# Gate pieces of a token group at other half steps of the dense layers, in a chain of attention, dense layers and a mixture of experts

## The chip, the core and the metric

One core of a Trainium2 chip runs the whole program. The metric is the device time of one execution, in microseconds (us). The engines are named as the profile names them: PE (TensorE, the matrix engine) and PEld (its weight loads), DVE (VectorE), ACT (ScalarE), POOL (GpSimd), SP (SyncE, which here only issues DMAs).

## The reference

Three stages follow one another on 4608 tokens of width 512. The attention stage works in chunks of 64 tokens; the dense stage is two layers; the last is a mixture of 8 experts with a noisy gate that picks two of them for each token.

```python
attn = softmax(scale * q_c @ k_c.T);  x = attn @ v_c          # chunks of 64 tokens, 8 heads of 64
...
h = x @ w_in                                                   # 512 -> 2048
x = (h - np.tanh(h)) @ w_out                                   # 2048 -> 512
...
noise_scale = np.log1p(np.exp(x @ w_noise))
noisy_logits = x @ w_gate + noise_scale * noise
top2 = ...                                                     # two largest of 8, softmax weights
for e in range(E):
    out[mask] += top2_w[mask] * (relu(x[mask] @ w1[e]) @ w2[e])  # 512 -> 1024 -> 512
```

## The kernel before

**Tiling.** The 4608 tokens are 36 tiles of 128. They form 11 groups g0 to g10 of 4 or 3 tiles (4, 3, 4, 3, 4, then 3 each). The dense layers of a group run in 16 steps, one for each 128 columns of the hidden layer, and each step has two half steps: the first layer (`layer1`, 12 matmuls of L327 into `hp`, which has two buffers) and the second layer of the step before (`layer2`, three matmuls for each tile, L399, into `acc`, four PSUM banks). So a group has 32 half steps, numbered 0 to 31; an even one is behind a first layer, an odd one behind a second. Numbers are 32-bit floats split in a high and a low part, three passes each. Between the layers `activate` forms h - tanh(h): the tanh on ACT (L347), the subtraction on DVE (L350), the cast of the high part on ACT (L351), the low part on DVE (L353). The second layer of the step needs both parts, and L350 also frees the bank of `hp`.

**What runs beside them.** Each half step has a list of other work (`at(h, fn, ...)`), which is recorded behind that half step's matmuls and what follows them, on all engines. The order within an engine is the order of recording; nothing rearranges it. In these lists stand the attention of later tiles (`u_attn` and its softmax pieces, L172 to L180 on DVE), the loads and transposes of tiles of x, and the gate of the group before: while group g is in its dense layers, the gate of group g-1 is computed. Its pieces are `u_lg` (logits on PE), `u_gate` (L487 on, exp), `u_gate2` (start of the series for log1p), `u_gate2a` (the series: eight terms in L519, the last in L520, all on DVE), `u_gate2b` (noise and top-2, L528 to L537 on DVE), `u_gate2c` (exp on ACT), `u_gate3` (weights and one-hot, POOL and DVE) and `u_pos` (place of each token in its expert's list, two matmuls and ten DVE operations, then the scatters).

**Scatters.** `u_pos` puts into the queue `waiting` one `reload` for each tile, and behind those the short entries of the lists. A `reload` loads a tile `yr` from `x2d` and puts a pair of scatters of it, `xs<-yr` (L602), into `loaded`. `issue`, called twice in each step, lets them out: POOL copies a mark into `spacer` (L376), which waits until ACT (L369) or DVE (L371) has written that mark in `activate`, then sends all that is in `loaded`, then takes one thunk from `waiting`. The ACT mark is only written when something waits at that time.

**End of a group.** The second layer of the last step runs inside the first step of the next group. Behind it `store_y` copies the banks of `acc` into tiles `y`, even ones on ACT (L443), odd ones on DVE (L441), and SP stores them to `x2d` (L444). Later `u_z` and `u_yt` load and transpose them for the gate. The tiles `y`, `z`, `x2t`, `yr` and `o` share one ring of four buffers (the tag "y"), so each waits until the last reader of the buffer is done.

Of the kernel before, what the change touches and what calls it, by code (L numbers as in the profile page):

```python
# [15 lines left out]
ALU = mybir.AluOpType  # L16
# [14 lines left out]
def moe_chain_kernel(ctx: ExitStack, tc: tile.TileContext, q, k, v, w_in, w_out, wgn, noise,  # L31
                     w1, w2, out):
    nc = tc.nc
    NT = q.shape[0]
    NTOK = NT * 128
    GS = SIZES or [4, 3] * 3 + [3] * ((NT - 21) // 3)
    NG = len(GS)
# [392 lines left out]
    GT = {}  # L430
# [70 lines left out]
    def u_gate2(g):  # L501
# [11 lines left out]
        ve.tensor_scalar(u, s2, 2.0 / (2 * n_terms + 1), None, op0=ALU.mult)  # L513
        GT[g] = lg, u, t, s2, n_terms, nz

    def u_gate2a(g):
        lg, u, t, s2, n_terms, nz = GT[g]
        for m in range(n_terms - 1, 0, -1):
            nc.vector.scalar_tensor_tensor(u, u, 2.0 / (2 * m + 1), s2, op0=ALU.add, op1=ALU.mult)  # L519
        nc.vector.scalar_tensor_tensor(u, u, 2.0, t, op0=ALU.add, op1=ALU.mult)  # L520
        GT[g] = lg, u, nz
# [350 lines left out]
    def L(f, *a):  # L872
        return lambda: f(*a)
# [107 lines left out]
    def at(h, fn, *a):  # L981
        slots[h].append(L(fn, *a))
# [15 lines left out]
    for g in range(1, NG - 1):  # L998
        hs = (1, 5, 9, 14, 18, 23) if g == 1 else (5, 9, 15, 21) if GS[g + 1] > 3 else (5, 14, 20)
# [11 lines left out]
    for g in range(NG):  # L1011
        h0 = H1 * g
        at(h0, load_nz, g)
        if g > 0:
            n = GS[g - 1]
            for j in range(n):
                i = G0[g - 1] + j
                at(h0 + 1 + j, u_z, i)
                at(h0 + 5 + j, u_yt, i)

            h = h0 + (11 if g + 1 < NG and GS[g + 1] > 3 else 9)
            at(h, u_lg, g - 1)
            h += 2
            for d, fn in zip((0, 2, 3, 4, 6, 7, 12), (u_gate, u_gate2, u_gate2a, u_gate2b,
                                                      u_gate2c, u_gate3, u_pos)):
                at(h + d, fn, g - 1)
        if g == 0:
            at(H1 + 6, sums)
            at(26, store_consts)
            for o, f in ((0, 3), (1, 2), (1, 3)):  # L1030
                at(0, fetch_w, o, f)
            for f in range(NF1):
                at(2 * f, fetch_w, 0, f + 4)
                if f:
                    at(2 * f, prep_w, 1, f)
                at(2 * f, decode_w, 0, f + 2)
                at(2 * f, rebias_w, 0, f + 3)
                at(2 * f + 1, fetch_w, 1, f + 4)
                at(2 * f + 1, prep_w, 0, f + 2)
                at(2 * f + 1, decode_w, 1, f + 1)  # L1040
                at(2 * f + 1, rebias_w, 1, f + 2)
        else:
            for f in range(0, NF1):
                if g == 1:
                    if f < E:
                        at(h0 + 2 * f, zero_x, 2 * f)
                        at(h0 + 2 * f, zero_x, 2 * f + 1)
                elif (g - 2) * NF1 + f < NT + DUMMY // 128:
                    at(h0 + 2 * f, zero_out, (g - 2) * NF1 + f)
        if g == NG - 1:  # L1050
            at(h0 - 4, u_cum)
            at(h0 - 2, u_bump)
            at(h0 + 12, load_list0)
            for c in range(min(3, SEAL // 128)):
                at(h0 + 8 + 3 * c, fetch_x, 0, c)
            for c in range(g0[1]):
                at(h0 + min(21 + 4 * c, H1 - 1), first_xt, c)
            for f in range(NF2):
                at(h0 + 2 * f + 7, fetch_e, 0, f)
                at(h0 + 2 * f + 10, prep_e, 0, f)  # L1060
# [26 lines left out]
    for gi, (e, ge, c0, nt, n) in enumerate(groups):  # L1087
        h0 = H1 * NG + H2 * gi
        if gi == 0:
            for j in range(GS[-1]):  # L1090
                at(h0 + 1, u_z, G0[-1] + j)
                at(h0 + 6 + j, u_yt, G0[-1] + j)
            at(h0 + 6 + GS[-1], u_lg, NG - 1)
            h = h0 + 8 + GS[-1]
            for d, fn in zip((0, 1, 1, 2, 3, 3), (u_gate, u_gate2, u_gate2a, u_gate2b,
                                                  u_gate2c, u_gate3)):
                at(h + d, fn, NG - 1)
            at(h + 4, u_cum)
            at(h + 7, u_pos, NG - 1)
            at(h0 + H2 + 3, u_over)  # L1100
            at(h0 + H2 + 7, dispatched)
            at(h0 + 2 * H2 + 2, load_list)
        if gi + 1 == len(groups):
            at(h0 + 8, u_tiles_over)
        else:
            for j in range(groups[gi + 1][3]):
                at(h0 + ((3 + 2 * j, 10 + 2 * j)[gi] if gi < 2 else 1 + 4 * j), xt_unit, gi + 1, j)
        if ge < 2:
            for f in range(4):
                at(h0 + 4 * f, fetch_e, e + 1, 4 * ge + f)  # L1110
                at(h0 + 4 * f + 3, prep_e, e + 1, 4 * ge + f)
# [72 lines left out]
```

## Time and profile before

| | us |
|---|---|
| three runs | 1760.42, 1760.86, 1760.87 |
| median | 1760.86 |
| span of the profiled execution | 1760.4 |
| PE busy in it | 1739.3 (99%) |
| PEld busy | 1489.6 (85%) |
| DVE busy | 791.3 (45%) |
| ACT busy | 547.1 (31%) |
| POOL busy | 492.9 (28%) |

The span is that of one execution, from its first to its last instruction. Matmuls are pipelined, so blocks of them overlap a little in the timeline; how far a block is late is read from the distance between the starts of two blocks. Idle time of the other engines costs nothing unless PE comes to wait for it.

### The profile page before, as it was taken

Reading aid. Unit: us, or ns where it says so; the run is one execution under the profiler, and the core shown is the slowest. Engines: PE = TensorE matmul, PEld = TensorE weight load, DVE = VectorE, ACT = ScalarE, POOL = GpSimd, SP = SyncE. Lnnn points to the kernel's source line nnn. Section 1 sums busy time; section 2 is a strip of 40 time slices with the busy share of each in tenths; the row PEclk is TensorE's granted clock in tenths of the full one; section 3 lists DMA queues with packets and bytes.
Section 4 is the critical chain, followed back from the end, with each engine's and each line's share of the span. In section 5 each row is a group of like instructions: output and inputs, shape, how many; then the busy total and the mean of one; then the engine's idle time right before and its main releaser. Section 6 shows DMA issues by size and latency. Waiting matters only on the chain. (4 is left out here: it accounts for less than half of the span.)

```text
span 1760.4 us, 28384 instructions
## 1 busy us (share of the span) xinstructions
PE 1739.3 (99%) x10791; PEld 1489.6 (85%) x10792; DVE 791.3 (45%) x2070; ACT 547.1 (31%) x1108; POOL 492.9 (28%) x752
## 2 busy tenths in 40 slices
PE   8999999999999999999999999999999999999997
PEld 5788888888888888888888888988898888988886
DVE  7966453645354545544466333433333333343321
ACT  4643322332233323332343323233223223232211
POOL 3650403040304123031353523222232223132112
PEclk9999999999999999999999999999999999999999
DMA  7436435562314222230354543443343343343212
GB/s 292 182 117 176 151 83 143 134 175 66 106 59 137 67 79 91 73 103 25 120 161 114 141 107 78 101 108 65 88 103 102 73 95 91 84 119 71 55 25 36
DMA packets 197830, 184.68 MB, mean 105 GB/s; under 512 B 80176, under 2 KB 139568, under 8 KB 197680
## 3 DMA queue, kind: packets, MB, share of 16 engines
q1 hardware_dynamic: 178064, 142.73, 27.1%
q0 software_dynamic: 19328, 39.41, 11.3%
q8 instruction: 96, 1.57, 0.4%
q10 hardware_dynamic: 288, 0.52, 0.1%
q14 instruction: 54, 0.44, 0.1%
HBM read 118.76 MB, written 63.84 MB: 104 GB/s over the span
## 5 line engine op out<-in xcount | busy, mean ns | idle before, releaser
L327 PE MATMUL hp<-xt,wa 128*128 128x384 f32 (+3 forms) x4416 | 885.5, 349 | 0.6 <-DVE g L350 0.6
L399 PE MATMUL acc<-wb,gt 128*128 128x512 f32 (+1 forms) x3510 | 877.9, 395 | 2.9 <-ACT gt L351 2.4
L327 PEld LDWEIGHTS hp<-xt,wa 128*128 128x128 f32 x4416 | 766.9, 188 | 83.6 <-issue 2.2
L399 PEld LDWEIGHTS acc<-wb,gt 128*128 128x128 f32 (+1 forms) x3510 | 650.2, 188 | 139.3 <-ACT gt L351 3.7
L358 DVE SCALAR_TENSOR_TENSOR gt<-hp,gt 128x384 fp32r<-128x384 f32 (+2 forms) x192 | 113.5, 591 | 469.1 <-ACT gt L355 453.7
L355 ACT ACTIVATE gt<-hp 128x384 fp32r<-128x384 f32 (+2 forms) x192 | 99.4, 518 | 476.9 <-PE hp L327 416.4
L350 DVE TENSOR_TENSOR g<-hp,g 128x384 f32<-128x384 f32 (+1 forms) x176 | 103.8, 590 | 257.7 <-ACT g L347 235.4
L347 ACT ACTIVATE g<-hp 128x384 f32<-128x384 f32 (+1 forms) x176 | 91.5, 520 | 335.2 <-PE hp L327 303.3
L312 POOL TENSOR_TENSOR wb<-st,wb 128x512 fp32r<-128x512 f32 x64 | 92.8, 1451 | 323.1 <-ACT wb L310 323.1
L351 ACT CAST gt<-g 128x384 fp32r<-128x384 f32 (+1 forms) x176 | 95.4, 542 | 164.2 <-DVE g L350 134.4
L376 POOL COPY spacer<-mark 1x1 f32<-1x1 f32 x182 | 46.7, 257 | 346.9 <-DVE mark L371 280.6
L353 DVE TENSOR_TENSOR gt<-g,gt 128x384 fp32r<-128x384 f32 (+1 forms) x160 | 94.8, 592 | 96.1 <-ACT gt L351 86.3
L732 POOL DMA_INDIRECT out_dram<-o,lsa x73 | 119.3, 1634 | 56.7 <-DVE o L729 37.9
L551 POOL TENSOR_SCALAR r<-d 128x3 f32<-128x3 f32 (+1 forms) x11 | 5.1, 461 | 388.5 <-ACT d L542 388.4
L602 POOL DMA_INDIRECT xs<-yr,row x72 | 71.5, 993 | 32.0 <-issue 24.2
L269 DVE TENSOR_TENSOR xt<-xg,xt 128x512 fp32r<-128x512 f32 x80 | 54.3, 679 | 54.4 <-ACT xt L268 53.7
L268 ACT CAST xt<-xg 128x512 fp32r<-128x512 f32 x80 | 48.8, 610 | 93.3 <-DVE xg L449 86.8
L602 POOL DMA_INDIRECT lst<-pay,row x72 | 70.1, 974 | 16.7 <-issue 15.6
L449 DVE STREAM_TRANSPOSE xg<-xg 128x512 f32<-128x512 f32 x80 | 56.4, 704 | 0.0
L312 DVE TENSOR_TENSOR wa<-st,wa 128x512 fp32r<-128x512 f32 x64 | 45.2, 706 | 5.4 <-ACT wa L310 5.3
L310 ACT CAST wa<-st 128x512 fp32r<-128x512 f32 x64 | 39.2, 613 | 4.5 <-DMA st<-in_w_dram 4.5
L310 ACT CAST wb<-st 128x512 fp32r<-128x512 f32 x64 | 39.7, 620 | 0.2 <-DMA st<-in_w_dram 0.2
(195 smaller groups left out, 864.3 us busy)
## 6 DMA issues: line engine op xcount, KB each, us to landing
st<-in_w_dram SPq DMA_DIRECT2D x128, 256.0 KB
xg<-xs SPq DMA_DIRECT2D x320, 64.0 KB
out_dram<-zero SPq DMA_DIRECT2D x40, 256.0 KB
x2d<-y SPq DMA_DIRECT2D x36, 256.0 KB
z<-x2d SPq DMA_DIRECT2D x144, 64.0 KB
yr<-x2d SPq DMA_DIRECT2D x36, 256.0 KB
q<-in_q_dram SPq DMA_DIRECT2D x34, 256.0 KB
v<-in_v_dram SPq DMA_DIRECT2D x34, 256.0 KB
```

What stands on the lines that cost most here:

```text
L310: nc.scalar.copy(w[:, 0, :], x)
L312: eng.tensor_tensor(w[:, 1, :], x, w[:, 0, :].bitcast(F32), op=ALU.subtract)
L327: nc.tensor.matmul(s.hp[:, :m], lhsT=w[:, a, d, :], rhs=s.xt[:, b, d, :m], start=(i == 0), stop=(i == 11))
L347: nc.scalar.activation(g, hp[:, :n], AF.Tanh)
L350: nc.vector.tensor_tensor(g, hp[:, :n], g, op=ALU.subtract)
L351: nc.scalar.copy(hi, g)
L353: eng.tensor_tensor(lo, g, hi.bitcast(F32), op=ALU.subtract)
L355: nc.scalar.activation(hi, hp[:, :n], AF.Relu)
L358: nc.vector.scalar_tensor_tensor(lo, hp[:, :n], 0.0, hi.bitcast(F32), op0=ALU.max, op1=ALU.subtract)
L399: nc.tensor.matmul(s.grp["acc"][j][:m], lhsT=s.gt[:, a, j * 128:j * 128 + m], rhs=s.B[s.f][:, b, :], start=(s.f == 0 and i == 0), stop=(s. ...
L602: s = nc.gpsimd.indirect_dma_start(out=to, out_offset=bass.IndirectOffsetOnAxis(ap=at, axis=0), in_=src, in_offset=None)
L732: a = nc.gpsimd.indirect_dma_start(out=out, out_offset=bass.IndirectOffsetOnAxis(ap=en[:m, 0:1], axis=0), in_=o[:m], in_offset=None, compu ...
```

## The change

The series of `u_gate2a` is cut: a new piece `u_gate2h` does its first four terms, and `u_gate2a` the other four and the last, by the number of terms left. The pieces of the gate stand at other half steps. In the order logits, gate, gate2, gate2h, gate2a, gate2b, gate2c, gate3, pos the half steps were 11, 13, 15, -, 16, 17, 19, 20, 25 for g1 and g3, and 9, 11, 13, -, 14, 15, 17, 18, 23 for the others; now they are in four rows, one each for g10, g1, g3 and the rest. The expert phase, which runs the gate of g10, keeps its own table.

```diff
         n_terms = 9
         ve.tensor_scalar(u, s2, 2.0 / (2 * n_terms + 1), None, op0=ALU.mult)
         GT[g] = lg, u, t, s2, n_terms, nz
+
+    def u_gate2h(g):
+        lg, u, t, s2, n_terms, nz = GT[g]
+        for m in range(n_terms - 1, n_terms - 5, -1):
+            nc.vector.scalar_tensor_tensor(u, u, 2.0 / (2 * m + 1), s2, op0=ALU.add, op1=ALU.mult)
+        GT[g] = lg, u, t, s2, n_terms - 4, nz
 
     def u_gate2a(g):
         lg, u, t, s2, n_terms, nz = GT[g]
@@
-            h = h0 + (11 if g + 1 < NG and GS[g + 1] > 3 else 9)
-            at(h, u_lg, g - 1)
-            h += 2
-            for d, fn in zip((0, 2, 3, 4, 6, 7, 12), (u_gate, u_gate2, u_gate2a, u_gate2b,
-                                                      u_gate2c, u_gate3, u_pos)):
-                at(h + d, fn, g - 1)
+            if g == NG - 1:
+                hs = (9, 11, 12, 14, 16, 18, 20, 20, 23)
+            elif g == 1:
+                hs = (11, 12, 13, 21, 22, 26, 28, 29, 31)
+            elif GS[g + 1] > 3:
+                hs = (11, 12, 13, 18, 19, 24, 26, 28, 30)
+            else:
+                hs = (9, 11, 12, 13, 17, 18, 21, 24, 28)
+            for h, fn in zip(hs, (u_lg, u_gate, u_gate2, u_gate2h, u_gate2a, u_gate2b, u_gate2c,
+                                  u_gate3, u_pos)):
+                at(h0 + h, fn, g - 1)
```

The first place is DVE in the middle of group 3 (the gate of group 2). Before, from the series on; L172 to L180 are the softmax of an attention tile, L528 to L535 the top-2 piece, which goes on with three more pairs of L534 and L535 and L537 before the next L350:

```order
L519 SCALAR_TENSOR_TENSOR u<-u,s_3804 128x32 x8
L520 SCALAR_TENSOR_TENSOR u<-u,t 128x32
L172 TENSOR_REDUCE sm<-e 128x8
L176 TENSOR_SCALAR sm<-sm 128x8
L177 RECIPROCAL sm<-sm 128x8
L180 TENSOR_TENSOR e<-e,sm 128x512
L528 SCALAR_TENSOR_TENSOR u<-lg,u 128x32
L529 TENSOR_TENSOR u<-u,nz 128x32
L530 TENSOR_TENSOR u<-u,lg 128x32
L534 MAX m_3856<-u 128x8
L535 MAX_INDEX i_3857<-m_3856,u 128x8
```

Now, from the softmax of one attention tile on; the lines of the kernel are 6 further down behind the new function:

```order
L177 RECIPROCAL sm<-sm 128x8
L180 TENSOR_TENSOR e<-e,sm 128x512
L350 TENSOR_TENSOR g<-hp,g 128x384
L353 TENSOR_TENSOR gt<-g,gt 128x384
L371 MEMSET mark 1x1
L519 SCALAR_TENSOR_TENSOR u<-u,s_3724 128x32 x4
L525 SCALAR_TENSOR_TENSOR u<-u,s_3724 128x32 x4
L526 SCALAR_TENSOR_TENSOR u<-u,t 128x32
L350 TENSOR_TENSOR g<-hp,g 128x384
L353 TENSOR_TENSOR gt<-g,gt 128x384
L371 MEMSET mark 1x1
L211 TENSOR_TENSOR xt_3491<-pair,xt_3491 128x2x4x64
```

Between the softmax, the series (L519, L525, L526) and the top-2 piece, which comes three steps later, now stands at least one whole row of L350, L353 and mark.

The second place is DVE at the end of group 6, from the last operations of `u_pos` to the copy of the next `y` (L441, in the first step of group 7). Before:

```order
L596 SCALAR_TENSOR_TENSOR fl<-lo__7426,hi__7428 128x6
L598 SCALAR_TENSOR_TENSOR row<-ef,pi 128x6
L599 SCALAR_TENSOR_TENSOR row<-ef,fl 128x6
L350 TENSOR_TENSOR g<-hp,g 128x384
L353 TENSOR_TENSOR gt<-g,gt 128x384
L371 MEMSET mark 1x1
```

Four more rows of L350, L353 and mark (the rest of the group's steps and the next group's first) stood before the next L441. Now:

```order
L602 SCALAR_TENSOR_TENSOR fl<-lo__7507,hi__7509 128x6
L604 SCALAR_TENSOR_TENSOR row<-ef,pi 128x6
L605 SCALAR_TENSOR_TENSOR row<-ef,fl 128x6
L350 TENSOR_TENSOR g<-hp,g 128x384
L353 TENSOR_TENSOR gt<-g,gt 128x384
L371 MEMSET mark 1x1
L350 TENSOR_TENSOR g<-hp,g 128x384
L353 TENSOR_TENSOR gt<-g,gt 128x384
L371 MEMSET mark 1x1
L441 COPY y<-acc 128x512
```

Two such rows are left between `u_pos` and the copy of `y`, where five were.

## Rows read from the trace of the kernel before

**Rows 1.** page, part 1: busy us, share of the span, instructions:
```profile
PE 1739.3 (99%) x10791; PEld 1489.6 (85%) x10792; DVE 791.3 (45%) x2070; ACT 547.1 (31%) x1108; POOL 492.9 (28%) x752
```

**Rows 2.** timeline of PE: start us, us, engine, line, operation, [idle before <-releaser]:
```profile
173.48 2.36 PE L399 MATMUL acc<-wb,gt 128*128 128x512 f32 x9
176.42 1.83 PE L327 MATMUL hp<-xt,wa 128*128 128x384 f32 x9 [0.58 <-DVE g L350]
...
348.88 2.27 PE L327 MATMUL hp<-xt,wa 128*128 128x384 f32 x12
352.79 2.37 PE L399 MATMUL acc<-wb,gt 128*128 128x512 f32 x9 [1.64 <-ACT gt L351]
...
885.63 2.28 PE L327 MATMUL hp<-xt,wa 128*128 128x384 f32 x12
888.42 2.36 PE L399 MATMUL acc<-wb,gt 128*128 128x512 f32 x9 [0.51 <-ACT gt L351]
```

**Rows 3.** timeline of VectorE (DVE) ahead of the gap at 352.79:
```profile
346.06 1.55 DVE L519 SCALAR_TENSOR_TENSOR u<-u,s 128x32 f32<-128x32 f32 x7
...
348.92 0.69 DVE L180 TENSOR_TENSOR e<-e,sm 128x512 f32<-128x512 f32 x1
349.52 0.18 DVE L528 SCALAR_TENSOR_TENSOR u<-lg,u 128x32 f32<-128x32 f32 x1
...
351.64 0.55 DVE L350 TENSOR_TENSOR g<-hp,g 128x384 f32<-128x384 f32 x1
```

**Rows 4.** timeline of ScalarE (ACT) at the same place:
```profile
352.22 0.51 ACT L351 CAST gt<-g 128x384 fp32r<-128x384 f32 x1 [4.74 <-DVE g L350]
```

**Rows 5.** timelines of VectorE and GpSimd (POOL) ahead of the gap at 888.42:
```profile
882.18 2.60 DVE L519 SCALAR_TENSOR_TENSOR u<-u,s 128x24 f32<-128x24 f32 x7
...
882.58 1.30 POOL L312 TENSOR_TENSOR wb<-st,wb 128x512 fp32r<-128x512 f32 x1 [3.15 <-ACT wb L310]
```

**Rows 6.** timeline of PE over the boundary from group 5 to group 6:
```profile
547.50 2.25 PE L399 MATMUL acc<-wb,gt 128*128 128x512 f32 x9
...
551.70 2.26 PE L399 MATMUL acc<-wb,gt 128*128 128x512 f32 x9
553.80 2.27 PE L327 MATMUL hp<-xt,wa 128*128 128x384 f32 x12
555.91 0.63 PE L399 MATMUL acc<-wb,gt 128*128 128x512 f32 x2
557.10 1.90 PE L399 MATMUL acc<-wb,gt 128*128 128x512 f32 x7 [0.56 <-issue]
```

**Rows 7.** timeline of ScalarE over the same boundary:
```profile
552.29 0.17 ACT L369 COPY mark<-zero 1x1 f32<-1x1 f32 x1
...
553.43 0.58 ACT L443 COPY y<-acc 128x512 f32<-128x512 f32 x1
556.46 0.58 ACT L443 COPY y<-acc 128x512 f32<-128x512 f32 x1 [2.44 <-PE hp L327]
```

**Rows 8.** timeline of GpSimd, the scatters ahead of that boundary:
```profile
539.18 0.17 POOL L376 COPY spacer<-mark 1x1 f32<-1x1 f32 x1
...
542.38 0.18 POOL L376 COPY spacer<-mark 1x1 f32<-1x1 f32 x1
...
545.57 0.18 POOL L376 COPY spacer<-mark 1x1 f32<-1x1 f32 x1
...
547.81 0.96 POOL L602 DMA_INDIRECT xs<-yr,row  x1 [0.23 <-issue]
```

**Rows 9.** windows: us, busy of each engine, PEclk, DMA share, GB/s:
```profile
549.50:550.00 0.50, 0.50 (x5) 0.46 (x4) 0.42 (x2) 0.00 (x0) 0.50 (x1) 1.00 1.01 393
550.00:550.50 0.50, 0.50 (x5) 0.50 (x4) 0.00 (x0) 0.00 (x0) 0.34 (x3) 1.00 0.04 8
```

**Rows 10.** timelines of ScalarE and PE in group 10, a later step:
```profile
900.44 0.51 ACT L351 CAST gt<-g 128x384 fp32r<-128x384 f32 x1 [0.84 <-DVE g L350]
...
901.29 2.26 PE L399 MATMUL acc<-wb,gt 128*128 128x512 f32 x9
```

## Prediction

> **What bounds the kernel now.** I read the page's busy shares first: TensorE (PE) is busy 1739.3 us of a 1760.4 us span [rows 1], so a change pays or costs only by what it does to the gaps in the row of matmuls. Next the timeline of PE, looking for blocks that start later than the block before them explains. In the dense layers a half step (12 matmuls of L327, or 9 of L399) starts 2.1 us after the one before when nothing is late: 547.50, 551.70 and 555.91 are two half steps apart [rows 6]. The profiled execution's span is 1760.4, the lowest of the three runs shown and 0.46 under their median of 1760.86; the sum below is made on the span and 0.4 is added at the end.
>
> Three gaps belong to the pieces that the diff moves. In group 3's steps L399 starts 3.91 after L327 instead of 2.1 (348.88, 352.79): **1.8 lost**. In group 1's, L327 starts 2.94 after L399 (173.48, 176.42): **0.8**. In group 10's, L399 starts 2.79 after L327 (885.63, 888.42): **0.7** [rows 2]. VectorE's timeline says why: seven terms of the series take 1.55 from 346.06, the softmax pieces of attention follow until 349.5, then the top-2 piece, and only at 351.64 comes the subtraction L350 that the next half step needs, 5.58 after the seven terms began [rows 3]. ScalarE's cast L351 idles 4.74 for it [rows 4]. In group 10 the same seven terms, on narrower tiles, take 2.60 while GpSimd runs L312 for 1.30 [rows 5]. So the gap is a sum of work standing in one step, not one slow instruction.
>
> A fourth gap stands at the boundary from group 5 to 6. L399 of the new group does two matmuls at 555.91, and the third starts at 557.10, where 0.47 after 555.91 was its turn (nine in 2.1): **0.7 lost** [rows 6]. ScalarE shows the reason: the last copy of a y tile out of PSUM (L443) started only at 556.46 and ended at 557.04 [rows 7]. So the new group's third matmul goes when a y copy of the old group ends.
>
> **What the change removes.** No instruction is added: four series terms and four more plus the last are the same nine. In groups 1 and 3 the pieces stand in steps apart from the softmax pieces and from each other. The heaviest of what is left, top-2, is the stretch from 349.52 to 351.64, 2.1 us, against the 5.58 that made the gap; softmax alone is shorter still. I take both gaps as gone: 1.8 + 0.8 = 2.6, at the least 1.8 if the smaller stays. In group 10 the series stands apart from top-2, minus 0.7. PE's own small matmuls of the gate are moved from behind one layer to behind the other; I take +0.2 for that in all, between 0 and 0.5.
>
> Group 10 also gets a piece back. There the exp and the weights piece now share slot 20, and VectorE's reciprocal waits for GpSimd, which waits for the exp. They land in the step in which the expert phase's first tile is transposed. In that step the cast L351 starts at 900.44 and the L399 that reads it at 901.29, after 0.51 of the cast: 0.34 to spare [rows 10]. I estimate the cost at 1.1 to 2 us: three or four small operations of about 0.18 (as L528 in rows 3), 0.6, and a wait of 0.5 for the exp and a small step on GpSimd, or of 1.3 when an L312 stands there [rows 5]. Less the 0.34 that is 0.8 to 1.7, and 0 if the step's other work gives way; I take **+0.9**.
>
> **What the change adds: the scatter pieces at the boundary.** u_pos moves from slot 23 (25 in groups 1 and 3) to 28 (30 and 31). It queues, for each tile, a reload yr of that tile and two scatters of it into xs. These are let out by marks: a spacer copy on GpSimd waits for a mark, the loaded pair goes, then one reload. After slot 28 the first reload goes with the mark of step 14, the first pair with ScalarE's mark of step 15, the next pair with VectorE's mark of step 15, the third with the next group's first mark. The yr tiles come from the ring of four buffers that y, z and x2t use too, and store_y, in the next group's first step, writes its y copies into buffers that hold yr tiles still being scattered. In the kernel before, the pairs went five or six half steps earlier and were out of the way.
>
> Call P the start of step 14's L399 at such a boundary (547.50 in group 5). From rows of before I lay the new order on it. ScalarE's mark ends 552.46, 0.76 after its neighbour block's start at 551.70 [rows 6, 7]; with the hand-over I take 0.9. Pairs follow one another every 3.20 (539.18, 542.38), and the second scatter starts 2.24 after the spacer (545.57, 547.81) [rows 8]. After the last one started at 547.81 the DMA engines were full until 550.0 and nearly idle from there (shares 1.01 and 0.04) [rows 9], so it was out 2.2 to 2.7 after its start. Pair 0 is then out by P + 0.9 + 2.24 + 2.7 = **P + 5.85**, pair 1 by **P + 9.05**, pair 2 by **P + 12.25**; with 2.2 each is 0.5 earlier.
>
> The third matmul of the new group's first L399 has its turn at P + 4 x 2.1 + 0.47 = P + 8.88 (556.38 in rows 6, which is 0.72 before 557.10). What it waits for is a y copy (boundary n is the one from group n to n + 1):
> Boundaries 6 to 9 (three tiles to three): y1 goes into yr0's buffer, y2 into yr1's. y2 ends at 9.05 + 0.58 + 0.15 of hand-over = P + 9.78. **0.9 each, 3.6**.
> Boundary 5: y0, y1, y2 go into yr0's, yr1's, yr2's. The third matmul waits for y1 (0.9). Then y2 holds ScalarE until P + 12.9, so the tanh (taken as long as the cast), the subtraction and the cast of step 1 are late: 12.9 + 0.5 + 0.6 + 0.5 = P + 14.5 [rows 3, 4], where L399 of step 1 has its turn at 8.4 + 0.9 + 4.2 = P + 13.5, and starts on the cast's end. Another 0.9 or so: **1.8**, in place of the 0.7 there now.
> Boundaries 1 and 3 (three tiles to four): u_pos is 2 or 3 half steps later still, so pair 0 waits for the next group's mark and lands at P' + 5.85, counted from step 15's L399. y2 needs that buffer and ends at P' + 6.5; the fourth matmul, which waits for it, has its turn at 2.1 + 2.8 + 0.7 = P' + 5.6 (a half step on four tiles taken as four thirds of 2.1). **0.9 each, 1.8**.
> Boundaries 2 and 4 (four to three): half steps are longer, only the last copy, on VectorE behind pair 2, is late: **0.2 each, 0.4**.
> Together 7.6; with landing 0.5 sooner 3.9, with landing later see below. Queued behind the waiting copies are, on ScalarE, the tanh and the cast of the new group's step 1, on VectorE the subtraction of that step; I counted them where they bite. The store of y and the load of z shift by about 3 us with the copies; transposes of z come two steps later and have that room.
>
> A rule of the Trainium skill (page "DMA: Bandwidth & Descriptors", section "Anatomy of one DMA — SWDGE (gpsimd) path") speaks against the change: a DMA from GpSimd signals only when its last byte is confirmed in the target memory, with a fixed part of about 2 us for that. By its fit a scatter of 256 KB takes 2.6 us as an estimate, inside my 2.2 to 2.7 if it runs from the scatter's start; if it runs from the issue's end, it gives the third rival below.
>
> **The sum.** 1760.4 - 2.6 - 0.7 - 0.7 + 0.2 + 0.9 + 7.6 = 1765.1; with 0.4 for the median and rounding, **1765.5**.
>
> **The rivals.**
> (1) *The buffers are free in time*, so the copies do not wait. It decides at pair 1 being out by P + 8.15, 0.9 sooner than I reckon, which a shorter pair cadence before busy GpSimd work would give. For it: the copies at 552 to 557 leave half a step of room; against: the 3.20 repeats for every pair. Then only the removals count, and a cheap group 10: 1760.4 - 2.6 - 0.7 - 0.7 + 0.4 = **1756.8**, faster.
> (2) *Half of it*: landings at the early end (2.2), so boundaries 1 to 4 hide in the longer steps and the others cost 0.5 or so, or the gate's gaps stay in part. 4 x 0.5 + 1.4 for boundary 5 in place of 7.6 gives 1765.5 - 4.2 = **1761.3**, no change that can be measured.
> (3) *Release comes later than the bytes*: the rows show bytes moving, not the buffer's release. If release counts from the end of the issue (547.81 + 0.96) [rows 8], every landing is 0.96 later. Nine boundaries at 0.96 more: 1765.5 + 8.6 = **1774.1**. Against it: the engines were idle from 550.0 on; for it: no engine is seen to wait for a scatter in the trace of before, so no row shows a release.
> (4) *The change does nothing to PE's gaps of groups 1 and 3*, because another piece takes the place of the moved one: 1765.5 + 2.6 = 1768.1. Little speaks for it, since 2.1 us of work fits in a step.
>
> **How the numbers follow.** Forecast 0.56, rival 1 0.11, rival 2 0.17, rival 3 0.10, rival 4 0.06. What a measurement can tell from no change is about 0.2%, that is 1757.3 and 1764.4. Of the forecast, which spreads over about 2 us to either side, a quarter lies under 1764.4. Faster: most of rival 1, 0.09. Same: rival 2, a quarter of the forecast and the rest of rival 1, 0.33. Slower 0.58. The range from 1757.5 to 1770 leaves out rival 3 and most of rival 1.
>
> **What would show it.** On PE: no start over 2.4 after the one before in groups 1 and 3 around slots 13 to 28; a gap of about 0.9 inside the first L399 of groups 7 to 10 (third matmul), two of them at group 6. On ScalarE: L443 of y2 starting about 2.5 us late, with the scatter as what released it. On GpSimd: scatters of xs on both sides of each boundary. If the copies start on time while scatters stand there, the step with the landing is wrong; if L443 is late by more than 3.5, rival 3 holds; if a gap is left in group 3, the step on VectorE's load is wrong.

## The result, and the profile after

The changed kernel takes **1778.2 us** (1777.39 to 1779.07) against 1760.86 before: ratio 1.0097, 95% interval 1.0086 to 1.0109. Slower was forecast, but by 4.6 us, and it is 17.3. In two later measurements the same kernel took 1804.7 and 1802.6, where the kernel before took 1762.3 and 1762.1, so 42 and 40 over it; the experiments show what most of those 24 us more are.

The profiled execution of the first measurement has a span of 1775.6, 15.2 over that of before. PE is busy 2.4 longer than before [rows 1], so most of the time went into gaps. First part 1 of the page of after, then its table of waits of PE, and two lines of its table of all waits (engine, tile, line, what was waited for: us in total, times, longest us):

```profile
PE 1741.7 (98%) x10788; PEld 1490.1 (84%) x10792; DVE 791.4 (45%) x2070; ACT 547.2 (31%) x1108; POOL 492.0 (28%) x752
```

```profile
PE acc L399 <- ACT y L443: 11.4, 8, 2.3
...
PE acc L399 <- DVE y L441: 1.5, 1, 1.5
...
PE pair L581 <- POOL mk L572: 0.8, 1, 0.8
```

```profile
DVE y L441 <- DMA xs<-yr,row: 15.6, 5, 5.5
...
ACT y L443 <- DMA xs<-yr,row: 12.9, 4, 5.9
```

The first two lines are the second layer of a group waiting for the y copies of the group before, 12.9 us in nine waits; the last two name scatters of yr as what nine y copies of this kernel waited for. In the trace of before L399 waited 2.4 in all for the cast L351, and no y copy is put down to a scatter of xs. Not every copy that PE waited for has the scatter named beside it (711.80 to 715.97 below says "issue"); that the buffers are the cause in all of them is shown by experiments 2 and 10. The gaps of groups 1 and 3 [rows 2] are gone; PE's timeline of after at the two places shows half steps 2.19 and 2.11 apart:

```profile
172.53 2.35 PE L399 MATMUL acc<-wb,gt 128*128 128x512 f32 x9
174.72 2.27 PE L327 MATMUL hp<-xt,wa 128*128 128x384 f32 x12
...
348.37 2.27 PE L327 MATMUL hp<-xt,wa 128*128 128x384 f32 x12
350.48 2.25 PE L399 MATMUL acc<-wb,gt 128*128 128x512 f32 x9
```

One boundary in full, from group 7 to 8: the timelines of PE, of ScalarE, of GpSimd and of SyncE's queue.

```profile
705.87 2.25 PE L399 MATMUL acc<-wb,gt 128*128 128x512 f32 x9
...
714.28 0.63 PE L399 MATMUL acc<-wb,gt 128*128 128x512 f32 x2
716.61 1.67 PE L399 MATMUL acc<-wb,gt 128*128 128x512 f32 x6 [1.71 <-ACT y L443]
```

```profile
711.80 0.58 ACT L443 COPY y<-acc 128x512 f32<-128x512 f32 x1
715.97 0.58 ACT L443 COPY y<-acc 128x512 f32<-128x512 f32 x1 [3.59 <-issue]
```

```profile
710.10 0.17 POOL L376 COPY spacer<-mark 1x1 f32<-1x1 f32 x1
...
712.33 1.00 POOL L608 DMA_INDIRECT xs<-yr,row  x1 [0.21 <-issue]
```

```profile
712.41 4.50 SPq L444 DMA_DIRECT2D x2d<-y  x3
```

P is 705.87. The second scatter of pair 1 starts at 712.33 = P + 6.46 (forecast 6.34). The y copy that waits for its buffer starts at 715.97, 3.64 later, and PE's third matmul goes at 716.61, when the copy has ended. Its turn was 714.28 + 0.47 = 714.75, so 1.86 is lost. The windows show the DMA engines at shares of 0.75 to 1.00 from 712.5 to 715.5 (us, busy of each engine, PEclk, DMA share, GB/s): the stores of y0 and y1, which SyncE sends as soon as those copies end, run ahead of the scatter's bytes and among them.

```profile
712.50:713.00 0.50, 0.50 (x5) 0.50 (x4) 0.50 (x1) 0.00 (x0) 0.50 (x1) 1.00 0.91 344
...
714.50:715.00 0.50, 0.41 (x2) 0.00 (x0) 0.00 (x0) 0.00 (x0) 0.50 (x1) 1.00 1.00 381
715.00:715.50 0.50, 0.00 (x0) 0.00 (x0) 0.00 (x0) 0.00 (x0) 0.36 (x2) 1.00 0.98 365
```

The longest wait is at the boundary from group 1 to 2, and it costs twice. The timeline of PE, and windows behind the gap:

```profile
209.45 0.86 PE L399 MATMUL acc<-wb,gt 128*128 128x512 f32 x3
212.59 3.91 PE L399 MATMUL acc<-wb,gt 128*128 128x512 f32 x9 [2.28 <-ACT y L443]
216.34 0.85 PE L327 MATMUL hp<-xt,wa 128*128 128x512 f32 x3
```

```profile
212.00:213.00 1.00, 0.41 (x2) 0.34 (x3) 0.00 (x0) 1.00 (x3) 0.51 (x2) 0.94 0.42 160
213.00:214.00 1.00, 1.00 (x4) 0.81 (x3) 0.69 (x1) 0.30 (x3) 0.27 (x2) 0.50 0.96 358
...
216.00:217.00 1.00, 1.00 (x5) 0.84 (x4) 0.00 (x0) 0.00 (x0) 0.00 (x0) 0.85 0.57 215
```

After 2.28 us without a matmul the granted clock is 0.50 (the lower of its two levels, 1.2 GHz), and nine matmuls take 3.75 from start to next start where they take 2.1 [rows 6]: 1.65 more. Behind the boundary from 9 to 10 another 1.0 goes in the same way, after 2.12; behind that from 3 to 4, after 2.02, the clock stayed at 1.00.

### The profile page after: what moved, and what is told of

It is laid out like the page before. It is cut to its first block, busy times and chain, and to the rows that moved or that the text cites. A ratio compares the mean times of both kernels' runs of the same rounds, so it can differ in the third digit from the quotient of the medians.

```text
span 1775.6 us, 28388 instructions
## 1 busy us (share of the span) xinstructions
PE 1741.7 (98%) x10788; PEld 1490.1 (84%) x10792; DVE 791.4 (45%) x2070; ACT 547.2 (31%) x1108; POOL 492.0 (28%) x752
## 5 line engine op out<-in xcount | busy, mean ns | idle before, releaser
L399 PE MATMUL acc<-wb,gt 128*128 128x512 f32 (+1 forms) x3510 | 883.6, 396 | 14.7 <-ACT y L443 11.4
L399 PEld LDWEIGHTS acc<-wb,gt 128*128 128x128 f32 (+1 forms) x3510 | 650.5, 188 | 155.3 <-ACT y L443 14.8
L350 DVE TENSOR_TENSOR g<-hp,g 128x384 f32<-128x384 f32 (+1 forms) x176 | 103.8, 590 | 258.5 <-ACT g L347 257.6
L351 ACT CAST gt<-g 128x384 fp32r<-128x384 f32 (+1 forms) x176 | 95.4, 542 | 140.2 <-DVE g L350 118.3
L353 DVE TENSOR_TENSOR gt<-g,gt 128x384 fp32r<-128x384 f32 (+1 forms) x160 | 94.3, 590 | 96.0 <-ACT gt L351 96.0
```

The lines of the kernel that those rows point to most:

```text
L350: nc.vector.tensor_tensor(g, hp[:, :n], g, op=ALU.subtract)
L351: nc.scalar.copy(hi, g)
L353: eng.tensor_tensor(lo, g, hi.bitcast(F32), op=ALU.subtract)
L399: nc.tensor.matmul(s.grp["acc"][j][:m], lhsT=s.gt[:, a, j * 128:j * 128 + m], rhs=s.B[s.f][:, b, :], start=(s.f == 0 and i == 0), stop=(s. ...
```

## The experiments

In each, time is the median, beside the kernel before on the same chip. Theory A is that of the prediction: y copies wait for buffers whose scatters are not released.

**1. u_pos alone late**, on the kernel before.

```diff
+                if fn is u_pos and g < NG - 1:
+                    at(h0 + (31 if g == 1 else 30 if g == 3 else 28), fn, g - 1)
+                else:
+                    at(h + d, fn, g - 1)
```

> The kernel before, with u_pos alone moved to where the change puts it (31 for group 1, 30 for group 3, 28 for the others; group 10 stays at 23). Theory A, that the loss comes from y copies that wait for buffers whose scatters are not released yet: all boundary stalls of the changed kernel appear, some 14 us of waits in eight boundaries and 2 to 3 us of half clock behind the longest, and the two gaps of groups 1 and 3 stay. So 1760.9 + 16 = 1777, at the least 1774. Theory B, that the new places of the other pieces cost it: within 1759 to 1763.

1802.1 against 1762.6. So u_pos alone makes a loss as large as that of the changed kernel later on (experiments 5 and 13), and theory B falls; but 40 is far more than A gives. PE's waits name the rest:

```profile
PE pair L136 <- issue: 9.8, 19, 1.1
PE acc L399 <- ACT y L443: 8.5, 4, 2.5
```

The first line is new: the 64x64 matmuls of attention (L136) stand still 19 times, with no wait that the profile shows ("issue"). No such gap is in the first trace of the changed kernel.

**2. Buffers of its own for yr**, on the changed kernel (the y copies then have no scatter to wait for).

```diff
+    yrs = sp.tile([128, 2, 512], F32, name="yr", tag="bd", bufs=3)
...
-            y = blk("yr", "y", 4)
+            y = yrs[:, j % 2] if g < NG - 2 else blk("yr", "y", 4)
```

> The changed kernel, with the tiles yr of groups 0 to 8 in a buffer pair of their own (the third buffer of tag bd, idle until group 10) in place of the ring that the y copies use. Scatters stand where the change puts them, at the group boundaries. Theory A: the y copies have nothing to wait for, the third matmul goes on time, 18 us of stalls leave the changed kernel's span of 1775.6, so 1757 to 1759. Rival C, that scatters at the boundary cost by themselves (their bytes against the stores of y, GpSimd against VectorE): more than half of the loss stays, over 1768.

1808.2 against 1762.6. The waits for y are gone from the table, as A says, and the time is worse than ever: attention stands still 44 times.

```profile
PE pair L137 <- issue: 24.8, 44, 1.4
```

(The kernel has one line more, so L136 reads L137.) With no y wait to push it back, the attention visit at slot 5 falls more squarely into the burst that follows a boundary.

**3. Pieces spread, u_pos early.** Groups 1 and 3 with pieces in steps apart and u_pos at 25; the others as before, group 10 as in the change.

```diff
-                hs = (11, 12, 13, 21, 22, 26, 28, 29, 31)
+                hs = (11, 12, 13, 17, 19, 22, 23, 23, 25)
...
-                hs = (11, 12, 13, 18, 19, 24, 26, 28, 30)
+                hs = (11, 12, 13, 14, 18, 19, 20, 22, 25)
...
-                hs = (9, 11, 12, 13, 17, 18, 21, 24, 28)
+                hs = (9, 11, 13, 14, 14, 15, 17, 18, 23)
```

> The changed kernel's split series and its table for group 10; in groups 1 and 3 the pieces in steps apart but u_pos back at 25, in the other groups the places of the kernel before with u_pos at 23. Theory A: no boundary stall but the one at group 5 to 6 that the kernel before has (0.7), and the gaps of groups 1, 3 and 10 gone (0.8, 1.8, 0.7 and 0.3): 1760.9 - 3.5 = 1757.4. Theory B: no better than 1760, since pieces were moved.

1761.1 against 1762.6, ratio 0.9989 (0.9980 to 0.9998). No boundary waits for a scatter, attention runs. 1.3 of the expected gain went to a new wait, `PE pair L581 <- POOL mk L572` in group 1: the second matmul of u_pos came too close behind the piece that GpSimd computes for it.

**4. u_pos between the two** (28, 27, 26).

```diff
-                hs = (9, 11, 12, 13, 17, 18, 21, 24, 28)
+                hs = (9, 11, 12, 13, 17, 18, 20, 22, 26)
```

(groups 1 and 3 as in experiment 3, with 28 and 27 at the end)

> As the one before, but u_pos at 28 for group 1, 27 for group 3 and 26 for the others, so one step (4.2 us) sooner than the change has it and one and a half later than before. Theory A, with the release measured in the changed kernel (3.1 to 3.8 us from the second scatter's start): pair 1 is released by P + 6, pair 2 by P + 9.2, so only a copy behind pair 2 (boundary 5) can be a little late and the time is 1757 to 1759. If the loss grew with the distance moved, as a cost of scatters among other work would, it is about 1767.

1772.4 against 1762.6: a miss for theory A as I had sized it. Two things were in it. At the boundary from group 1 to 2 a full wait is left, since the gate there is that of group 0 with four tiles, and a copy's buffer was behind the third pair. Its second scatter starts at 209.78 and the copy at 212.81, 3.03 later. PE's timeline:

```profile
210.14 0.95 PE L399 MATMUL acc<-wb,gt 128*128 128x512 f32 x3
213.45 3.46 PE L399 MATMUL acc<-wb,gt 128*128 128x512 f32 x9 [2.36 <-issue]
```

The other boundaries have no such wait (0.2 at most), but attention stands still, 3.4 us in six times, five of them behind the boundary from 4 to 5.

**5. The changed kernel again**, on the chip of experiments 6 to 8.

> The changed kernel once more, on the chip of the next three, for comparison with the two runs above in which matmuls of attention stood still. If that standstill hangs on u_pos being late alone, it shows here too and the time is 1790 or more; if it hangs on where the burst of loads and scatters falls against the attention visit at slot 5, the y copies' waits push that visit behind the burst here, and the time is 1776 to 1780.

1804.7 against 1762.3. So experiment 1 and the changed kernel are alike, and the standing still belongs to the change. The order of scatters, loads and attention around a boundary is the same in this trace as in the first one; there attention ran through.

**6 and 7. Attention visits at other slots**, on experiments 2 and 1.

```diff
-        hs = (1, 5, 9, 14, 18, 23) if g == 1 else (5, 9, 15, 21) if GS[g + 1] > 3 else (5, 14, 20)
+        hs = (1, 5, 9, 14, 18, 23) if g == 1 else (8, 12, 16, 21) if GS[g + 1] > 3 else (9, 14, 20)
```

> The changed kernel with yr in its own pair of buffers, as in the second experiment, and the attention visits of groups 2 and later at other slots: 9, 14, 20 in place of 5, 14, 20, and 8, 12, 16, 21 in place of 5, 9, 15, 21 in group 3. Theory D, that the 64x64 matmuls of the visit at slot 5 starve because the loads of z, the scatters and the list entries run in the same microseconds: the 25 to 35 us of standing still there go, and with the y copies free as well (theory A) the time is 1757 to 1761. Theory E, that they starve for another reason that comes with late scatters: over 1780.

> The first experiment (the kernel before with u_pos alone late) with the attention visits moved in the same way. Theory D: the 14 us in the visit at slot 5 and the half clock behind them go, the waits of the y copies (14 us and their half clock) stay: 1776 to 1781. Theory E: no change, about 1800.

1804.5 and 1812.6 against 1762.3. Both are spoiled by the edit: slot 9 is that of the gate's logits, which now wait for the PSUM bank that the attention visit uses. Waits of experiment 6:

```profile
PE pair L474 <- DVE e L157: 19.2, 7, 2.8
PE pair L137 <- issue: 5.7, 12, 1.2
```

What can be used is the second line, 24.8 before: attention still stands still, though by then (593 to 597 in the trace) the last load of z had been issued at 589. What was still going out was GpSimd's list entries. That made **theory F**: the entries, lst<-pay, not the loads.

**8. The buffer pair on the kernel before**, a control.

> The kernel before with yr in its own pair of buffers and nothing else changed. Theories A and D: its scatters are released long before the boundary, so no wait goes and none comes: 1760 to 1763, as before. If two buffers for yr in place of four cost by themselves (the reloads wait on SyncE, and the loads behind them), it is over 1768.

1766.2 against 1762.3 (1.0011 to 1.0031): 4 more, and not all of it is the pair's. In its trace two attention visits stand still beside list entries (1.4 us in four times); in the trace of before none does.

**9 and 14. List entries held back**, on the changed kernel. u_pos no longer queues them; one call that sends them all is queued at slot 9 of the next group but one.

```diff
+        if g < NG - 2:
+            HELD[g] = entries
...
+        if g > 1:
+            at(h0 + 9, u_lst, g - 2)
```

> The changed kernel with one thing more: the short entries of the lists (lst<-pay) of groups 0 to 8 are held back and sent together from slot 9 of the next group but one, when the attention visit at slot 5 is over; the scatters of xs stay at the boundary. Theory F, that the 64x64 matmuls of that visit starve just while GpSimd sends list entries: the standing still in attention goes (16 us and half clock behind it in the run of the changed kernel on this chip) and the waits of the y copies stay: 1774 to 1782. Theory D, loads of z and scatters: 1795 or more.

1777.7 against 1760.8, with no standing still in attention behind a boundary; the waits for the y copies are all there:

```profile
PE acc L399 <- ACT y L443: 12.3, 8, 2.3
```

Since the first measurement showed no standing still, it was run again beside the changed kernel (13), the buffer pair (15) and the reverse test (16), all four on one chip:

> The changed kernel a third time, beside the next three on one chip. Theory A alone, on a chip where attention does not stand still: 1777 to 1779. With standing still (theory F on a chip like that of the second group of runs): 1795 to 1810.

> The changed kernel with the list entries held to slot 9, again, on this chip. Theory F: 1775 to 1780 even where the changed kernel itself takes 1795 or more. If it follows the changed kernel up to 1795 or more, F is wrong.

The changed kernel 1802.6, with held entries **1785.3**, the kernel before 1762.1. In the changed kernel attention stands still for 10.4 us in 19 times (`PE pair L136 <- issue: 10.4, 19, 1.2`); with held entries 1.2 are left of it, in four times, and an attention visit behind a boundary reads as it should:

```profile
655.34 0.69 PE L136 MATMUL pair<-pts,v 64*64 64x64 f32 x32
655.86 0.65 PE L136 MATMUL pair<-ks,q 64*64 64x64 f32 x32
```

That is the direction of F, though 1785.3 is above what I gave it (1775 to 1780). In group 3 another wait of 1.6 came, of the gate's matmul L492 for a copy, and the block behind it took 3.7 in place of 2.1. The 1.2 that are left of the standing still fall into two visits (222.7 and 406.2) where no entry is out, but scatters of xs are: entries are not the only indirect DMAs that do it.

**10 and 17. Held entries and the buffer pair together.**

> The same, and yr in a pair of buffers of its own. Theories A and F together: neither y copies nor attention wait, so 1758 to 1766 (the control of the pair of buffers was 4 over the kernel before). If A is wrong, over 1775; if F is wrong, about 1800, as in the second experiment.

> The changed kernel with yr in a pair of buffers of its own and the list entries held to slot 9, again on another chip. Theories A and F together are the whole loss: within 3 of the kernel before beside it, on either side. Something more is in it on some chips: 5 or more over the kernel before.

1758.6 against 1760.8 (0.9976 to 0.9994) and 1758.4 against 1761.3 (0.9973 to 0.9992). With both causes away nothing of the loss is left, and what remains is the gain of the spread pieces. Experiments 9 and 10 ran side by side and differ by the buffer pair alone: 1777.7 against 1758.6, so the waiting y copies cost 19, which is the 17.3 of the first measurement and the 2 by which 10 is under the kernel before. Experiment 14 is 23 over the kernel before; there the wait of L492 and the rest of the standing still are in it. What 10 and 17 do not show is the price of the entries: the pair without held entries did not run beside either, and in their traces, as in that of 9, attention visits run through beside scatters of xs (eight of eight), where in 14 both stand still. For the entries 13 against 14 and experiment 16 stand.

**11 and 16. List entries alone late, on the kernel before.** All scatters of xs stay early; the entries go out from slot 4 (11) or slot 3 (16) of the next group but one.

> The kernel before, with the list entries alone held back, to slot 4 of the next group but one, so that they are sent while the attention visit at slot 5 runs; all scatters of xs are early, as before. Theory F: 2 to 5 us of standing still in each of seven or eight groups, so 1775 to 1800. Theories A and D: nothing late that anyone waits for, within 3 of 1762.

> The kernel before with the list entries alone held back, to slot 3 of the next group but one, one half step sooner than in the eleventh experiment, so that they are under way when the attention visit at slot 5 begins. Theory F, where the changed kernel stands still: 2 to 5 us in seven or eight groups, 1775 or more. On a chip without standing still, or if F is wrong: within 3 of the kernel before.

From slot 4: 1761.4 against 1760.8, no difference, where F had 1775 to 1800. There the entries begin while the attention visit ends (639.7, visit 639.1 to 640.1), so it did not try what it was meant to. From slot 3 they are under way when it begins (669.6, visit 673.1 to 678.6): **1816.2 against 1762.1**, the slowest kernel of all, with nothing changed but that these few bytes are sent later, and those of a group in one call. PE's waits, its busy time on the page, PE and GpSimd at one visit, and windows there:

```profile
PE pair L136 <- issue: 26.9, 40, 1.1
```

```profile
PE 1766.6 (97%) x10791; PEld 1510.6 (83%) x10792; DVE 792.3 (44%) x2070; ACT 545.8 (30%) x1084; POOL 490.2 (27%) x770
```

```profile
673.63 0.46 PE L136 MATMUL pair<-ks,q 64*64 64x64 f32 x7
675.23 0.33 PE L136 MATMUL pair<-ks,q 64*64 64x64 f32 x4 [1.14 <-issue]
676.65 0.33 PE L136 MATMUL pair<-ks,q 64*64 64x64 f32 x3 [1.09 <-issue]
678.07 0.80 PE L136 MATMUL pair<-ks,q 64*64 64x64 f32 x18 [1.08 <-issue]
```

```profile
674.65 0.96 POOL L602 DMA_INDIRECT lst<-pay,row  x1 [0.21 <-issue]
...
675.91 0.96 POOL L602 DMA_INDIRECT lst<-pay,row  x1 [0.21 <-issue]
```

```profile
674.00:675.00 1.00, 0.09 (x3) 0.00 (x0) 0.00 (x0) 0.00 (x0) 0.79 (x3) 1.00 0.01 1
...
678.00:679.00 1.00, 0.93 (x19) 0.81 (x19) 0.00 (x0) 0.09 (x1) 0.00 (x0) 0.50 0.00 0
```

PE gets a few matmuls every 1.42 us while GpSimd sends entries, one every 1.26; the last goes out until 676.87, and PE runs freely from 678.07. The DMA engines are idle (share 0.01): it is not bandwidth. Then the clock is at 0.50 for the dense matmuls that follow. So of the 54 about half is standing still (26.9) and half the same matmuls running longer (PE is busy 1766.6, before 1739.3).

**15. The buffer pair with entries where the change has them, again.**

> The changed kernel with yr in a pair of buffers of its own and the entries where the change has them, again. On a chip where attention does not stand still, theory A alone: 1757 to 1761, near the run that also held the entries. Where it does, theory F: 1795 or more.

1809.6 against 1762.1, as in experiment 2 and as F says: `PE pair L137 <- issue: 23.3, 40, 1.1`.

**12 and 18. A version that beats both.** Experiment 3 with group 1's pieces a little sooner.

```diff
-                hs = (11, 12, 13, 17, 19, 22, 23, 23, 25)
+                hs = (11, 12, 13, 15, 17, 20, 21, 22, 25)
```

> As the third experiment, but with group 1's pieces one to three half steps sooner (gate3 at 22 in place of 23, two steps ahead of u_pos), so that the matmul of u_pos does not wait 1.3 for GpSimd. Theory A: 1.3 less than there, so 1759.5 to 1760.5 beside a kernel before of 1762.5; if DVE's load in the step of top-2 and softmax makes a gap instead, the same as there.

> The version with the pieces of groups 1, 3 and 10 spread and u_pos left at 23 and 25, again on another chip. Its gain is that of PE's gaps and hangs on no burst at the boundary: 3 to 5 under the kernel before beside it. If it hung on the chip of the twelfth experiment: within 1.

**1756.7** against 1760.8 (ratio 0.9976, 0.9967 to 0.9985) and 1757.2 against 1761.3 (0.9977, 0.9968 to 0.9986). The wait of u_pos's matmul is gone; the two matmuls follow each other (trace of 12):

```profile
189.86 0.19 PE L580 MATMUL pair<-mk,lower 128*128 128x32 bf16 x1
189.90 0.18 PE L581 MATMUL pair<-mk,ones 128*128 128x32 bf16 x1
```

## Why the prediction was wrong, step by step

**The mechanism and the place were right**: u_pos alone, without the other pieces, makes the loss (experiment 1); the copies L443 and L441 wait for scatters, a matmul of the new group's first L399 with them; and with buffers of its own for yr these waits and 19 us are gone (9 against 10). The size was off in several terms, and one cause was not seen at all.

**The landing, the term that failed.** I read the end of the bytes from two windows, let a buffer be free 2.2 to 2.7 after its second scatter's start, and put 0.15 on the hand-over to the copy: 2.85 at most. Measured from that start to the start of the copy that waited, it was 2.94 to 3.78: 3.12 and 3.74 behind groups 1 and 3, 3.34 and 2.94 at group 5, 3.13, 3.64, 3.16 and 3.78 behind 6 to 9. The order of events up to the scatter's start was right within 0.15 at 6 to 8 and 0.5 late at 9. The DMA packets in the two traces split the rest. In the trace of before the scatter of 547.81 has its last packet out at 550.18, 2.37 after its start, well inside what I read. Now, behind group 6, the packets of such a scatter begin only when the store of y0 has ended (637.70 to 638.56) and end 2.62 after its start; behind group 7 they run among those of y1's store too and end after 2.9; over all these boundaries the end is at 2.4 to 3.2. And from the last packet to the start of the copy it is 0.5 to 0.6 where the profile names the scatter as what was waited for (group 5's two, 6 and 8), and up to 0.8 elsewhere, not 0.15. At group 5's last copy no store is in the way: the packets end at 2.37, and the copy starts at 2.94. So both parts of the term were too small: the bytes end later where stores of y run beside them, and the copy starts later behind the bytes. The trace of before does have one wait that ends on an indirect DMA, where the prediction counted none: the y copy at 851.68 is put down to a list entry, and it starts 0.8 behind that entry's last packet (850.85). The third rival ("release comes later than the bytes") had 3.66 for the landing and 1774.1 for the time; it was the nearest of my cases, and I gave it 0.10. By the Trainium skill (page "DMA: Bandwidth & Descriptors", section "Anatomy of one DMA — SWDGE (gpsimd) path") a transfer of 256 KB takes an estimated 2.6. Counted from the scatter's start every boundary here is above that, and counted from the issue's end, 0.96 later, 3.56 lies within the measured span.

**Boundary by boundary**, as the excess of the distance between starts on PE over its usual one: forecast 0.9 each for 1 and 3, measured 2.45 and 2.2; 0.2 each for 2 and 4, measured 1.1 and 1.0; 1.8 at 5, measured 2.1; 0.9 each for 6 to 9, measured 1.4, 1.9, 1.4 and 2.3. Together 15.8 in place of 7.6. Behind group 1 the second scatter itself was 1.1 later than I laid it (208.84, where P' is 204.56): the first one started late and took 1.56.

**The clock.** It was not in the sum. After the longest waits the granted clock was 0.50: 1.65 and 1.0, from the rows above, 2.7 together.

**What the change removes**: right. 1.8, 0.8 and 0.7 are gone, and so is a gap of 0.4 in group 10 (905.89 in the trace of before) that I had not counted.

**Group 10's +0.9**: wrong, nothing came of it. The weights piece found room in its step. In its place u_pos's matmul in group 3 waits 0.8 for GpSimd, since piece and matmul now stand two half steps apart where they stood five apart; I had put +0.2 on PE's small matmuls and not asked what they wait for.

So 15.8 + 2.7 + 0.8 - 3.7 - 0.7 (the old gap at group 5) = 14.9, of 15.2 by the spans. By the times it is 17.3. The difference comes from the profile of before: in every execution with both numbers the time is 1.6 to 2.1 above the span (1777.7 and 1775.6 here), so the span 1760.4 belongs to a time of some 1762.4, an estimate, and not to the median of 1760.86. In the prediction I took that span for one of the times; the 0.4 that I added for it changed nothing in the loss forecast.

**What was not seen**: moving u_pos moves its list entries too. They are queued behind the reloads, so they now go out in the first steps of the next group, over the attention visit at slot 5. The prediction has no term for the entries. In the later runs they cost about as much as the y copies: 17 between 13 and 14, and 54 in experiment 16.

**What stays open**: why the first measurement's trace of the changed kernel shows no standing still although entries and visit overlap there (entries start from 641.3 to 648.3, visit 647.0 to 648.2), and that in six visits, where in experiments 1 and 13 all six such visits stand still; and what PE lacks while it stands. The traces narrow it down: none of the some 500 attention visits in all 20 of them without an indirect DMA of GpSimd beside it stands still, so these DMAs are a condition, but not the only one. In the standing still of 673.6 to 678.1 in experiment 16 the trace has no packet of the two queues that load instructions, so no such load was under way there.

## What to carry to other kernels

When a step is moved, follow everything it queues, to the last small transfer, to where it will be sent, and look at what then runs beside it and which buffers it still holds. The time at which a buffer is free again is read from a wait that ends on it, not from the end of the bytes; where no trace shows such a wait, the price of the bound belongs into the range with a large chance. And of a change with two parts, the part that fills gaps can be kept without the part that moves a transfer: spreading the pieces gave 4 us, once u_pos stayed early.

## What the runs showed of the hardware that was not expected

Short indirect DMAs from GpSimd (128 entries of 8 bytes each) can make a run of small matmuls stand still for 1.1 us at a time, at a DMA share of 0.01 and with no wait in the trace; in one kernel this alone cost 54 us of 1762, half of it in the lower clock behind. It showed in three sets of runs and not in the first measurement, nor in experiments 9, 10 and 17 beside scatters of xs; the number of the chip does not sort them, since 9 and 10 bear the same one (8) as 13 to 16. Dense matmuls of the same kernels, twelve in 2.1 us, did not show it. An indirect scatter of 256 KB with nothing beside it had its last packet out 2.37 us after its start, and a copy that waited for it started 0.5 to 0.8 behind the last packet; stores sent just ahead of its bytes pushed that end to as much as 3.2. After 2.28 us without a matmul the granted clock was 0.50 for some 3 us; that is 1.65 on nine matmuls, in addition to the wait.
